# Block-sparse attention and a ResMLP in one kernel: pair 5's q and k transposed by DMA, the opening and the weave's lists placed anew

## The chip, the cores and the metric

The kernel runs on one core of a Trainium2 chip. The metric is the device time of one execution in microseconds. A core has five engines with instruction queues of their own: TensorE (PE; its weight loads are shown as PEld), VectorE (DVE), ScalarE (ACT), GpSimd (POOL) and SyncE (SP, which only issues DMAs here). POOL and SP issue nearly all DMAs; each executes its queue strictly in the order written.

## The reference

```python
def _attn_ref(q, k, v, sampled_blocks):          # q, k, v: 4 x 8 x 768 x 64
    scores = (1 / sqrt(D)) * q @ k.transpose
    mask = |block_i - block_j| <= 1 or first/last block row or column
           or one of 3 sampled blocks per row of blocks (blocks of 32)
    attn = softmax(where(mask, scores, -1e9))
    return attn @ v

def _moe_ref(x, ...):                            # x: 4 x 768 x 512, heads side by side
    a1 = alpha1 * x + beta1
    tok = einsum('ts,bsd->btd', w_tok, a1)
    u = x + lam * tok
    a2 = alpha2 * u + beta2
    ch = relu(a2 @ w_ch1) @ w_ch2                # 512 -> 2048 -> 512
    return u + lam * ch
```

## The kernel before

**Tiling.** The eight heads of each of the four batches are taken two by two: 16 *pairs* (`NP` = 4 to a batch). The scores of a pair are computed key by key in nine *units* (`WIDE`, `HALF`): a unit is 128 x 1024 scores in PSUM, two or four matmuls (`emit_qk`, L569), then one Exp of 1024 or two of 512 columns on ACT into a tile `eT` (`emit_exp`, L587; six such tiles). `emit_pv` (L616) and `emit_pv_keys` (L639) multiply the result with v (matmuls of 65 columns), `emit_finish` (L656, L657) divides, on VectorE, into `x_sb`, and `emit_a1pp` (L673, L674) makes `a1`, mostly on POOL.

**Two kinds of pairs.** Pairs 0 to 4 (`MP` = 5) carry the mask inside the matmul, with 24 more rows. Pairs 5 to 15 keep q and k of both heads on 64 rows each (`qhTs`, `khTs`), two matmuls run side by side, and the mask is a multiply on VectorE after the Exp (`emit_keep`, L604), for which POOL first spreads the mask out (`emit_mask01`, L505).

**Transposes.** q and k must stand with the head dimension on the partitions. Pair 0 goes through `emit_tps0` (L467), pairs 1 to 4 through `emit_tps` (L479, L485): six TensorE transposes into PSUM, then VectorE copies. Pairs 6 to 15 go through `emit_tdma` (L530 for k, L535 and L538 for q): DMA transposes on SP's queue. Pair 5 goes through `emit_tph` (L519; copies L521 and L524 to L526) or `emit_tdma`, as `TDM[1]` says (`TDM[0]` is read by nothing).

**The MLP.** `job_tok` and `job_tok2` multiply with the transposed `w_tok` (`emit_wtok_t`, L761) and add to `x_sb`; `emit_cast` makes bf16 copies; these are transposed by TensorE (`job_ut`, L829, L830) or by DMA (`emit_udma` L844, `emit_uscale` L853). `job_f1` (L867, four matmuls of 384 columns, then Relu on ACT, L874) and `job_f2` (L886, four matmuls of 512 columns; after four such jobs the add L895 and the store) are the channel MLP; 128 f1 jobs and 92 f2 jobs, and the last tile in two parts (L906). `w2b` is scaled by `lam` in 16 VectorE multiplies (`lam0` to `lam15`, L748).

**What sets the order.** `tc.manual_schedule()`: each engine executes in the order in which the code emits.

- *The opening*: 45 units, one after the other (pairs 0 to 4). In unit `s` the code emits the scores, the Exp, the jobs of `PLAN` whose number is `s` to `s`.49, from unit 42 on `POUR[s - 42]` f1 jobs, then the PV pieces of unit `s - 2`, then the jobs of `PLAN` from `s`.5. A number is a place in the order, no time.
- *The weave*: a list of strings for each third of a pair (`W1` for pairs 5 to 7, `W2` for four pairs and run twice, `W3` the tail). `q` emits three units' scores and the first Exp, `x` another Exp, `k` a mask multiply, `p` a PV piece, `f` and `g` an f1 and f2 job, `T` a `job_tok2`, `s` starts the MLP work of a finished couple of pairs, `d` and `v` are `emit_udma` and `emit_uscale`, `L` loads q, k and v of a later pair (POOL, L304), `Q` and `K` are the DMA transposes of the next pair, `Y` copies v (L315), `0`, `1`, `2` emit what `PLAN` holds for that place.
- `A1V` says for pairs 0 to 3 which `emit_a1pp` go to VectorE instead of POOL.
- `emit_warm` (L449) issues matmuls of 512 columns on a tile of zeros: eight ahead of everything, two more ahead of unit 0, and the jobs `warm0`, `warm1`, `warm2` (one, two and one).

PSUM has two tiles `sp` for scores, three `mm` for nearly everything else and one `op` for PV results and warm matmuls. The constants of each vector (`parts`, POOL, L696 to L700) are spread over the partitions by `emit_bcast` (L705, L714, L716).

```python
    for s in range(N1):
        emit_qk(s)
        emit_exp(s)
...
        fns(s, False)
        if s >= OPEN:
            for _ in range(POUR[s - OPEN]):
                todo["f"].pop(0)()
        if s >= LAG:
            emit_pvs(s - LAG)
        fns(s, True)
```

Of the kernel before, what the change touches and what calls it, by code (L numbers as in the profile page):

```python
# [71 lines left out]
]  # L72
WEAVE = W1 + W2 * (B - 2) + W3
ENG = {
# [19 lines left out]
    "layv00": 0.29,
    "wtkl": 0.42,
    "warm1": 0.49,
    "loadv2": 0.58,
    "layk01": 1.22,
    "layq01": 1.25,
    "mask_cols": 1.5,  # L100
    "rows1": 2.08,
    "tps0": 2.52,
    "parts": 2.83,
    "mask1": 2.94,
    "w1_0": 2.96,
    "warm2": 3.04,
    "warm0": 3.31,
    "tq1": 3.8,
# [1 line left out]
    "rows2": 4.5,  # L110
    "tk1": 4.82,
    "lv1": 5.01,
    "bcast0": 5.1,
    "rows3": 5.84,
    "loadk3": 6.08,
    "bcast2": 6.12,
    "loadv3": 7.02,
    "mask3": 7.41,
# [2 lines left out]
    "bcast1": 8.8,
    "loadq3": 9.23,
    "a1pp0": 9.37,
    "w1_2": 9.64,
    "w1_1": 10.3,
    "columns": 11.32,
    "wt2": 11.35,
    "wt1": 11.76,
    "wt5": 12.19,
    "lv2": 12.84,  # L130
    "wt4": 13.01,
    "wt0": 13.43,
    "loadv4": 13.94,
    "w1_3": 14.3,
    "tq2": 14.44,
    "loadq4": 14.54,
    "wt3": 15.31,
    "columns_use": 16.32,
    "tk2": 16.6,
    "tok0_0": 17.05,  # L140
    "tok0_1": 17.4,
    "tk3": 18.13,
    "loadk4": 18.23,
    "tok0_2": 20.0,
    "tq3": 20.4,
    "mask8": 20.72,
    "loadk5": 20.73,
    "mask2": 20.89,
    "tok0_3": 21.32,
    "tok0_4": 22.02,  # L150
    "lv3": 22.91,
    "mask6": 22.94,
    "mask0": 23.62,
    "tok0_5": 23.87,
    "loadq5": 24.3,
    "tok1_0": 24.53,
    "mask4": 24.64,
    "w2_0": 24.82,
    "mask7": 25.08,
    "lv4": 25.4,  # L160
    "tok1_1": 25.6,
    "tok1_2": 27.2,
    "loadv5": 27.53,
    "tok1_3": 27.74,
    "tok1_4": 28.91,
    "tok1_5": 29.7,
    "w2_2": 29.98,
    "mask5": 30.09,
    "tq4": 30.41,
    "mask15": 30.72,  # L170
    "udma0": 30.82,
    "tk4": 31.72,
    "udma1": 31.9,
    "w2_1": 32.02,
    "tq5": 32.51,
    "mask9": 32.65,
    "tok2_0": 33.91,
    "tk5": 34.64,
    "usc0": 34.69,
    "tok2_1": 34.88,  # L180
    "mask14": 34.9,
    "mask13": 35.48,
    "tok2_2": 35.71,
    "mask11": 35.79,
    "tok2_3": 36.37,
    "lam16": 37.24,
    "mask17": 37.68,
    "w2_3": 37.7,
    "mask16": 37.75,
    "tok2_4": 37.77,  # L190
    "mask10": 37.9,
    "tok3a_0": 38.34,
    "tok3a_1": 38.43,
    "tok2_5": 38.51,
    "tok3a_2": 38.52,
    "tok3a_3": 38.85,
    "tok3a_4": 39.48,
    "tok3b_0": 39.51,
    "tok3b_1": 39.52,
    "tok3b_2": 39.53,  # L200
    "tok3b_3": 39.54,
    "ut2": 39.85,
    "tok3a_5": 40.02,
    "mask12": 40.23,
    "tok3b_4": 40.23,
    "usc1": 40.28,
    "lv5": 40.42,
    "ut3_0": 40.8,
    "tok3b_5": 41.21,
    "cast3": 42.22,  # L210
    "lam2": 42.25,
    "lam3": 43.09,
    "ut3_1": 43.63,
    "lam1": 44.85,
    "lam10": 44.92,
    "lam9": 45.25,
    "lam7": 45.27,
    "lam0": 45.32,
    "lam11": 45.58,
    "lam6": 45.9,  # L220
    "lam13": 46.09,
    "lam5": 47.61,
    "lam14": 47.82,
    "lam4": 47.9,
    "lam8": 49.72,
# [6 lines left out]
def kernel(  # L232
# [416 lines left out]
    def emit_finish(i, w):  # L649
        b, hp = i // NP, i % NP  # L650
        if (hp, w) == (0, 0):
            x_sbs[b] = ap_.tile([P, NT, DM], FP, name="x_sb", tag="x_sb", bufs=3)
# [4 lines left out]
        nc.vector.tensor_tensor(  # L657
            out=x_sbs[b][:, :, ts(2 * hp + w, D)],
            in0=op[:, :, 0:D],
            in1=rcp[:].unsqueeze(2).broadcast_to([P, NT, D]),  # L660
            op=ALU.mult,
        )
# [520 lines left out]
```

## Time and profile before

| what | value |
|---|---|
| median of 3 runs | 303.80 us (303.79 to 303.88) |
| the profiled execution | 304.01 us |
| its span, first to last instruction | 302.2 us |
| busy in the span: TensorE, ACT, VectorE, POOL | 296.6, 214.5, 191.6, 111.6 us |
| granted TensorE clock | 1.00 |
| DMA moved | 31.37 MB, 104 GB/s mean |

The page gives busy times, the chain of work that ended last (followed back from the last instruction to what released each) and groups of instructions by line. Rows of the views name the line, the engine, the operation, the tile written and the tiles read, the count, and in brackets what ended an idle stretch of the engine. The end of a matmul is modelled, so TensorE counts as busy in short waits too; where its pieces in the chain are longer than their kind usually is, it waited. One execution was profiled; it lay 0.2 us over the median.

### The profile page before, as it was taken

The page shows a single profiled execution, that of the slowest core. Times are in us where ns is not written, and L with a number is a line of the kernel's source. Part 1 is how long each engine was busy: PE and PEld are TensorE (multiplying, and loading weights), DVE is VectorE, ACT ScalarE, POOL GpSimd, SP SyncE. Part 2 cuts the span into 40 slices and gives each one's busy share as a digit, 9 for nine tenths or more (in the row PEclk, how much of TensorE's full clock was granted, in tenths as well). Part 3 has the DMA queues.
Part 4 walks back from the last instruction along what each step waited for, and adds up shares of the span by engine and source line. Part 5 has one row for each costly group of instructions (what it writes and reads, how often), then busy time and mean ns, then how long its engine had stood idle before and what let it go on. Part 6 is the DMA issues. An engine that isn't in the chain of part 4 may idle for free.

```text
span 302.2 us, 7215 instructions
## 1 busy us (share of the span) xinstructions
PE 296.6 (98%) x2997; PEld 184.5 (61%) x2997; DVE 191.6 (63%) x373; ACT 214.5 (71%) x314; POOL 111.6 (37%) x147
## 2 busy tenths in 40 slices
PE   8999999999999999999999999999999999999995
PEld 3677888655567656565665556565675664555543
DVE  4887789887658899845477779854476872000012
ACT  4899997999879775889778774889868600663310
POOL 5989589344338432613407501603105300000000
PEclk9999999999999999999999999999999999999999
DMA  7999999827296797960746793880510004100011
GB/s 200 214 194 205 196 155 168 134 55 125 72 130 114 113 138 121 128 160 2 119 74 110 117 169 87 125 168 0 63 38 16 37 35 121 37 0 35 37 69 69
DMA packets 57891, 31.37 MB, mean 104 GB/s; under 512 B 37952, under 2 KB 54740, under 8 KB 57732
## 3 DMA queue, kind: packets, MB, share of 16 engines
q0 software_dynamic: 16608, 14.22, 32.1%
q1 hardware_dynamic: 40784, 16.15, 25.3%
q10 hardware_dynamic: 468, 0.55, 0.5%
q8 instruction: 23, 0.38, 0.5%
q14 instruction: 8, 0.07, 0.1%
HBM read 29.86 MB, written 6.29 MB: 120 GB/s over the span
## 4 chain that ended last, share of the span: by engine, by line
PE 96%; ACT 3%; issue 0%; DVE 0%
PE mm L867 28%; PE mm L886 27%; PE sp L569 10%; PE op L639 8%; PE mm L802 8%; PE mm L569 4%; PE mm L778 3%; ACT eT L587 3%; PE op L616 2%; PE op L449 2%; PE mm L906 1%; PE mm L616 1%; PE mm L479 1%; PE mm L761 1%; PE mm L829 0%
## 5 line engine op out<-in xcount | busy, mean ns | idle before, releaser
L587 ACT ACTIVATE eT<-sp,expb 128x1024 f16<-128x1024 f32 x111 | 118.3, 1117 | 4.4 <-PE sp L569 3.9
L874 ACT ACTIVATE hts<-mm 128x384 bf16<-128x384 f32 x128 | 62.0, 495 | 48.0 <-PE mm L867 47.2
L867 PE MATMUL mm<-uT,w1b 128*128 128x384 bf16 x512 | 92.6, 326 | 0.0
L604 DVE TENSOR_TENSOR eT<-eT,mask 128x1024 f16<-128x1024 f16 x99 | 74.1, 771 | 26.9 <-ACT eT L587 26.6
L886 PE MATMUL mm<-w2b,hts 128*128 128x512 bf16 x368 | 87.7, 379 | 0.0
L673 POOL TENSOR_TENSOR a1pp<-x_sb,vbc 128x384 bf16<-128x384 f32 x27 | 32.7, 1210 | 123.0 <-DVE x_sb L657 121.8
L867 PEld LDWEIGHTS <-w1b 128*128 128x128 bf16 x512 | 48.1, 98 | 35.0 <-issue 3.4
L886 PEld LDWEIGHTS <-hts 128*128 128x128 bf16 x368 | 34.1, 98 | 38.6 <-issue 4.0
L587 ACT ACTIVATE eT<-mm,expb 128x512 f16<-128x512 f32 x66 | 41.7, 685 | 18.6 <-PE mm L569 18.3
L895 DVE TENSOR_TENSOR ot<-x_sb,mm 128x512 f32<-128x512 f32 x23 | 15.7, 684 | 45.4 <-PE mm L886 45.4
L639 PEld LDWEIGHTS <-eT 128*128 128x128 f16 x792 | 29.6, 98 | 8.7 <-issue 1.5
L639 PE MATMUL op<-vext,eT 128*128 128x65 f16 x792 | 31.7, 194 | 0.0
L674 POOL TENSOR_TENSOR a1pp<-a1pp,vbc 128x384 bf16<-128x384 bf16 x27 | 27.8, 1029 | 2.1
L569 PE MATMUL sp<-qTs,kTs 88*128 88x512 bf16 (+1 forms) x120 | 27.1, 327 | 0.9 <-ACT eT L587 0.7
L802 PE MATMUL mm<-a1pp,wtokT 128*128 128x256 bf16 x216 | 25.6, 273 | 0.0
L802 PEld LDWEIGHTS <-wtokT 128*128 128x128 bf16 x216 | 20.7, 98 | 4.2 <-ACT hts L874 0.8
L569 PE MATMUL sp<-qhT,khT 64*128 64x256 bf16 (+1 forms) x176 | 19.7, 322 | 0.0
L616 PEld LDWEIGHTS <-eT 128*128 128x128 f16 x360 | 14.9, 97 | 4.2 <-PE op L449 0.8
L569 PEld LDWEIGHTS <-khT 64*128 64x128 bf16 x264 | 10.5, 94 | 10.8 <-issue 6.8
L814 DVE TENSOR_TENSOR x_sb<-x_sb,mm 128x512 f32<-128x512 f32 x18 | 12.3, 686 | 7.1 <-PE mm L802 6.8
L657 DVE TENSOR_TENSOR x_sb<-op,rcp 128x384 f32<-128x384 f32 x28 | 15.6, 557 | 1.0
L820 DVE CAST ubf<-x_sb 128x256 bf16<-128x256 f32 (+1 forms) x44 | 13.7, 347 | 0.9
(92 smaller groups left out, 222.8 us busy)
## 6 DMA issues: line engine op xcount, KB each, us to landing
out_dram<-ot SPq DMA_DIRECT2D x23, 256.0 KB, 2.0
qpad<-in_q_dram POOLq DMA_DIRECT2D x15, 192.0 KB, 4.0
kr<-in_k_dram POOLq DMA_DIRECT2D x15, 192.0 KB, 5.7
vr<-in_v_dram POOLq DMA_DIRECT2D x15, 192.0 KB, 6.0
w1b<-in_moe_w_ch_dram POOLq DMA_DIRECT2D x4, 512.0 KB, 10.3
w2b<-in_moe_w_ch_dram POOLq DMA_DIRECT2D x4, 512.0 KB, 7.4
hts<-in_moe_w_tok_dram POOLq DMA_DIRECT2D x1, 1152.0 KB, 10.4
x_sb<-in_k_dram ACTq DMA_DIRECT2D x2, 192.0 KB, 3.2
```

The costliest lines, as they stand in the source:

```text
L569: nc.tensor.matmul(sp[jj][:, dst], lhsT, rhs, start=True, stop=True, skip_group_check=True,)
L587: nc.scalar.activation(dst, at, AF.Exp, bias=expb[:], scale=SCALE)
L604: nc.vector.tensor_mul(out=e, in0=e, in1=keep)
L616: nc.tensor.matmul(op[0][:, o, :], ets[u][:, jj, h * QB + n * P : h * QB + n * P + P], vexts[i % NVB][:, w, 2 * jp + jj, :], start=op[1] == 0,
L639: nc.tensor.matmul(op[0][:, o, :], ets[u][:, jj, h * QB + n * P : h * QB + n * P + P], vexts[i % NVB][:, w, 2 * jp + jj, :], start=op[1] == 0,
L673: eng.tensor_tensor(out=dst, in0=x_sbs[b][:, :, cols], in1=bc[0], op=ALU.mult)
L674: eng.tensor_tensor(out=dst, in0=dst, in1=bc[1], op=ALU.add)
L802: nc.tensor.matmul(ps[:, o], wtokT[:, os_, ts(2 * n + o, P)], a1pps[i][:, os_, :], start=(os_ == 0 and o == 0), stop=(os_ == NT - 1 and o ...
L867: nc.tensor.matmul(ps[:, 0:QC], w1b[:, dk, ts(n, P)], uTs[b][:, dk, ts(c, QC)], start=(dk == 0), stop=(dk == 3),)
L874: nc.scalar.activation(hts[(b, c)][:, n, :], ps[:, 0:QC], AF.Relu)
L886: nc.tensor.matmul(ps[:], ht[:, nk, ts(o % 3, P)], w2b[:, nk, :], start=(nk == 0), stop=(nk == NH - 1),)
L895: nc.vector.tensor_tensor(out=ot[:], in0=x_sbs[b][:, o, :], in1=ps[:], op=ALU.add)
```

## The change

Pair 5's `tk5` and `tq5` call `emit_tdma`: three DMA transposes on SP's queue instead of twelve transposes on TensorE and four copies on VectorE. All else is a new order of the same instructions: `A1V` moves one `emit_a1pp` of pair 1 from POOL to VectorE or back (entry 0 is read by nothing; entries 2 and 3 change places), `POUR` emits no, nine and no f1 jobs in units 42 to 44 (a negative count is an empty range), the lists of the weave are written anew, and 131 of the 134 numbers of `PLAN` change.

```diff
-TDM = [1, 0]
-A1V = [1, 0, 0, 1, 0, 0, 0, 1]
-POUR = [3, 1, 1]
+TDM = [1, 1]
+A1V = [0, 0, 1, 0, 0, 0, 0, 1]
+POUR = [-21, 9, -78]
 W1 = [
-    "q f Y x f 0 f p k 1 f k f p x 2 f f k f f",
-    "q L f x Q f f f k p x f p 0 k 1 p k 2",
-    "q x g x f k k f 0 g 1 g k 2 K",
-    "q Y Q k p K g p x x 0 f 1 s k 2 p k L f",
-    "q 0 f x x g 1 g g k p k k 2",
-    "q k s g p f x 0 f k 1 T x f p 2 k",
-    "q 0 1 f p x k 2 p K T x L k p k",
-    "q f x f 0 x T 1 p 2 Y k p k k Q",
-    "q x f 0 k k g p x 1 s 2 g k d g",
+    "q Q f x 0 f f p f f 1 k f x f 2 f k p g k",
+    "q k 0 Y g g p p x 1 x K k 2 k",
+    "q g L 0 1 k x f f x p 2 s f f f k k p",
+    "q x k 0 p Y p K g x k g k L 1 2",
+    "q p g 0 s f p 1 x k x Q 2 g k k f T",
+    "q x p k T k x 0 1 f p 2 k f",
+    "q K T Q p d p s k L 0 1 2 x x k k f f",
+    "q f x f f k k g p p 0 x 1 f k Y g f p d g f 2",
+    "q 0 k g g x 1 x g f k 2 k",
 ]
 W2 = [
-    "q 0 p p p f d L x K f k v g 1 Q v g k x g g k 2",
-    "q x 0 k f x g s 1 k 2 T T p p k T",
-    "q d Y k p x g 0 1 2 g d g k x v p k",
-    "q k L g x k 0 p g g 1 x p k 2 Q v",
-    "q g x p g 0 x f f f Y k 1 f k 2 k f",
-    "q 0 f k p x k f p f f f x 1 p p K f k f 2",
-    "q f f x f f k 0 1 Q Y x p k g g 2 k s",
-    "q 0 g g s k x f f 1 f 2 x k L f k p p",
-    "q T f T T k 0 1 x x k K f f 2 f k p f f",
-    "q p p p d s k x L d 0 x K k g k Y 1 f f 2 g",
-    "q 0 x k Q g x 1 g p k 2 k p",
-    "q k x v 0 1 p g k x k f g f g 2",
+    "q 0 Q K v p p v x p x 1 g g k f k f k 2 Y f L s",
+    "q 0 x T T 1 k T g x p g 2 k k",
+    "q p 0 d 1 g k p g x k 2 x g d k",
+    "q k p p g K x g x v k k L p 0 v 1 2",
+    "q g k x 0 1 Y 2 k f f f f p p x f f k",
+    "q f 0 f k s x f p 1 f k f 2 x Q f f p f k f",
+    "q k Q 0 x k 1 p f Y g g L x 2 p k",
+    "q g x g f s 0 k 1 f k 2 x T K p p p k",
+    "q f x f 0 1 x f k T k k f p 2",
+    "q k T 0 p Q x k p L x 1 k s 2 f Y",
+    "q f K f k x g p 0 d g 1 g d x v k f k 2 g",
+    "q k v p p 0 1 x f f x 2 f g k g k",
 ]
 W3 = [
-    "p p p f g v f s g T T T g g d g g g g d g g v g v g g f f f f f f",
-    "f f f f f f f f f f f f g f f g f g f g f f g g f g f f g f f g g g f g",
-    "f f g g g g g g g g g g g g",
+    "p p p",
+    "f g s g T T T f d g v g g f d",
+    "g g g v g g g g g g f f f f f f f f g g f f g g f f f f f f f f g f f g f g g f f g f g g g f f f f f g g g f g f f g g g g g g g g",
 ]
```

Of `PLAN`, the entries that the prediction speaks of (before and after):

```diff
-    "warm1": 0.49,    "warm2": 3.04,    "warm0": 3.31,
+    "warm1": 27.17,   "warm0": 28.18,   "warm2": 44.07,
-    "bcast0": 5.1,    "rows1": 2.08,    "tps0": 2.52,    "parts": 2.83,
+    "bcast0": 4.68,   "rows1": 1.14,    "tps0": 2.99,    "parts": 2.39,
-    "loadk3": 6.08,   "loadv3": 7.02,   "loadq3": 9.23,  "a1pp0": 9.37,
+    "a1pp0": 9.68,    "loadq3": 9.8,    "loadv3": 9.93,  "loadk3": 10.27,
-    "w1_0": 2.96,     "w1_2": 9.64,     "w1_1": 10.3,    "w1_3": 14.3,
+    "w1_0": 15.3,     "w1_1": 29.93,    "w1_2": 34.16,   "w1_3": 37.56,
-    "tk3": 18.13,     "columns_use": 16.32,
+    "tk3": 21.97,     "columns_use": 28.85,
-    "udma0": 30.82,   "udma1": 31.9,    "tq5": 32.51,    "tk5": 34.64,
+    "udma0": 34.49,   "udma1": 35.98,   "tq5": 41.91,    "tk5": 41.99,
-    "usc0": 34.69,    "usc1": 40.28,    "ut2": 39.85,    "ut3_0": 40.8,   "ut3_1": 43.63,
+    "usc0": 38.06,    "usc1": 38.4,     "ut2": 41.67,    "ut3_0": 42.26,  "ut3_1": 44.2,
```

More of the change, by code (lines that the diff above doesn't have):

```diff
@@ L93 @@
 PLAN = {
[L94 to L108, printed above, removed]
-    "layv01": 4.3,
[L110 to L118, printed above, removed]
+    "wtkl": 0,
@@ L119 @@
+    "layk01": 0.2,
+    "layq01": 0.5,
+    "layv00": 0.6,
+    "loadv2": 0.95,
+    "rows1": 1.14,
+    "parts": 2.39,
+    "tps0": 2.99,
+    "mask_cols": 3.13,
+    "tq1": 3.23,
+    "layv01": 4.3,
+    "bcast0": 4.68,
+    "mask1": 4.85,
+    "rows2": 5.44,
+    "tk1": 6.79,
+    "bcast1": 7,
+    "mask14": 7.61,
     "loadk2": 8.21,
     "loadq2": 8.52,
[L121 to L225, printed above, removed]
@@ L226 @@
-    "lam12": 49.8,
-    "lam15": 50.13,
+    "mask12": 8.56,
+    "w2_0": 8.93,
+    "bcast2": 9.06,
+    "a1pp0": 9.68,
+    "loadq3": 9.8,
+    "mask16": 9.82,
+    "lv1": 9.89,
+    "loadv3": 9.93,
+    "loadk3": 10.27,
+    "mask2": 10.88,
+    "rows3": 10.97,
+    "wt2": 11.16,
+    "wt4": 11.97,
+    "lv2": 11.98,
+    "wt1": 12.42,
+    "wt0": 12.44,
+    "wt5": 12.97,
+    "tq2": 13.36,
+    "mask6": 14.26,
+    "wt3": 14.29,
+    "columns": 15.02,
+    "tk2": 15.18,
+    "w1_0": 15.3,
@@ new lines @@
+    "tok0_0": 16.7,
+    "tok0_1": 16.83,
+    "lv3": 17.04,
+    "loadv5": 17.17,
+    "loadq4": 17.24,
+    "mask11": 17.72,
+    "tok0_3": 18.08,
+    "w2_3": 18.19,
+    "loadv4": 18.38,
+    "mask0": 18.61,
+    "loadk4": 19,
+    "tok0_2": 19.49,
+    "tok0_4": 20.72,
+    "tok0_5": 20.74,
+    "tk3": 21.97,
+    "tq3": 22.12,
+    "loadq5": 22.27,
+    "w2_2": 22.78,
+    "w2_1": 23.21,
+    "tok1_0": 23.59,
+    "tok1_1": 24.32,
+    "loadk5": 24.33,
+    "tok1_3": 25.42,
+    "mask17": 25.92,
@@ new lines @@
+    "tok1_2": 25.97,
+    "warm1": 27.17,
+    "lam16": 27.45,
+    "lam13": 27.59,
+    "warm0": 28.18,
+    "columns_use": 28.85,
+    "lam15": 28.97,
+    "tok1_4": 29.02,
+    "mask15": 29.17,
+    "tok1_5": 29.17,
+    "mask10": 29.72,
+    "mask5": 29.8,
+    "w1_1": 29.93,
+    "lv5": 30.29,
+    "tk4": 31.06,
+    "mask8": 32.14,
+    "tok2_3": 32.57,
+    "lv4": 33.56,
+    "tok2_4": 33.78,
+    "tq4": 33.83,
+    "tok2_0": 33.99,
+    "w1_2": 34.16,
+    "tok2_1": 34.25,
+    "udma0": 34.49,
@@ new lines @@
+    "mask3": 34.73,
+    "tok2_2": 35.11,
+    "lam8": 35.56,
+    "udma1": 35.98,
+    "lam5": 37.36,
+    "mask9": 37.4,
+    "w1_3": 37.56,
+    "tok2_5": 37.65,
+    "tok3a_0": 37.97,
+    "usc0": 38.06,
+    "tok3a_1": 38.31,
+    "tok3a_3": 38.39,
+    "usc1": 38.4,
+    "tok3a_2": 38.69,
+    "tok3a_4": 38.91,
+    "tok3b_0": 40.29,
+    "tok3b_3": 40.34,
+    "tok3b_1": 40.5,
+    "tok3a_5": 40.62,
+    "tok3b_2": 40.75,
+    "mask4": 40.82,
+    "tok3b_4": 41.53,
+    "ut2": 41.67,
+    "tq5": 41.91,
@@ L228 @@
+    "tk5": 41.99,
+    "tok3b_5": 42.09,
+    "ut3_0": 42.26,
+    "lam10": 42.94,
+    "lam4": 43.19,
+    "lam9": 43.48,
+    "lam2": 43.54,
+    "cast3": 43.87,
+    "lam7": 43.91,
+    "warm2": 44.07,
+    "lam12": 44.09,
+    "ut3_1": 44.2,
+    "mask7": 44.23,
+    "mask13": 44.96,
+    "lam0": 45.45,
+    "lam3": 45.58,
+    "lam11": 46.99,
+    "lam1": 47.55,
+    "lam6": 47.81,
+    "lam14": 48.35,
 }
```

## The prediction

> **What bounds the kernel now.** I read three views: busy shares and the chain of work that ended last on the page, busy time by stretch, and the pieces of that chain in order of time.
>
> ```profile
> PE 296.6 (98%) x2997; PEld 184.5 (61%) x2997; DVE 191.6 (63%) x373; ACT 214.5 (71%) x314; POOL 111.6 (37%) x147
> ...
> PE 96%; ACT 3%; issue 0%; DVE 0%
> ```
>
> TensorE is busy 98% of the span and 96% of the chain is TensorE's. Busy is modelled there, so the stretches say more:
>
> ```profile
> 6.50:19.30 12.80, 11.82 (x156) 8.34 (x155) 10.62 (x28) 11.53 (x12) 11.01 (x21) 1.00 1.15 200
> 19.30:59.00 39.70, 39.67 (x651) 32.05 (x649) 34.14 (x71) 36.70 (x38) 30.98 (x45) 1.00 1.14 175
> 59.00:240.00 181.00, 181.00 (x1827) 109.34 (x1826) 130.62 (x238) 146.64 (x223) 65.54 (x68) 1.00 0.57 96
> ```
>
> The columns after the stretch are the busy times of PE, weight load, DVE, ACT and POOL. From 59 to 240 us (the weave) TensorE is busy 181.0 of 181.0, from 19.3 to 59 (the rest of the opening) 39.67 of 39.7. Before that it is not. The chain shows what bounds there:
>
> ```profile
> 6.93 2.13 ACT eT L587 x2
> ...
> 9.97 0.39 PE op L449
> ...
> 11.88 1.94 ACT eT L587 x2
> ...
> 13.92 0.80 ACT eT L587
> ...
> 15.91 2.25 ACT eT L587 x2
> ...
> 18.20 0.60 PE sp L569 x4
> 18.80 0.67 PE mm L761 x12
> 19.47 0.43 PE sp L569 x2
> ```
>
> Up to 18.2 us the chain runs over the Exp of L587, unit after unit; from 18.2 on it never leaves TensorE. So the rule for this change: up to 18 us what counts is when Exps can start; from there on, each TensorE instruction removed is time won, each one added is time lost, a reordering wins only where TensorE waits now, and it loses wherever a new wait appears.
>
> **The change part by part.**
>
> *Removed: 12 transposes of pair 5 (L519), with four VectorE copies.*
>
> ```profile
> 24.44 0.15 PE mm L729
> 24.60 0.44 PE mm L479 x6
> ...
> 28.46 0.59 PE sp L569 x4
> ...
> 34.72 0.59 PE sp L569 x2
> ...
> 39.07 0.50 PE sp L569 x2
> ...
> 42.10 0.34 PE mm L519 x6
> ...
> 43.77 0.34 PE mm L519 x6
> ...
> 54.02 1.95 PE mm L867 x12
> ```
>
> Both sixes stand in the chain with 0.34 us: **-0.68 us**. The copies are off the chain and count for nothing by themselves; VectorE was 34.14 of 39.7 busy there.
>
> *Added: three DMA transposes on SP's queue.* They stand behind the two of `udma0` and `udma1` and ahead of pair 6's.
>
> ```profile
> 34.31 7.18 SPq L844 DMA_TRANSPOSE uraw<-ubf  x2
> 57.73 1.21 SPq L535 DMA_TRANSPOSE qhT<-qpad  x1
> ...
> 30.99 0.72 POOL L304 DMA_DIRECT2D qpad<-in_q_dram  x1
> ...
> DMA to landing us min/median/max: 3.0/4.3/5.6
> ```
>
> SP runs ahead of TensorE: it is free from 41.5 to 57.7 us. Pair 5's q is fetched at 31 us (last row but one). So the three transposes go out from about 42 us, 1.2 us each, and with 5.6 us at most to land they are there by 52; the first matmul that needs them comes after 59. Nothing waits: 0. If that cover were gone (SP held up), each us beyond 59 would be a us of time.
>
> *Moved: four warm matmuls* (`warm0` to `warm2`, L449). Before, two stand behind unit 0's scores and two behind unit 3's, while TensorE waits anyway; now they stand in units 27, 28 and 44, inside the TensorE-bound stretch. A 512-column matmul there takes a quarter of the four in the next row's pace, 1.73 / 8 = 0.216 us:
>
> ```profile
> 74.50 1.73 PE mm L886 x8
> ```
>
> 4 x 0.216 = **+0.86 us**. What their leaving wins at the start is bounded by:
>
> ```profile
> 9.53 0.81 PE L449 MATMUL op<-warm 128*128 128x512 bf16 x2
> ...
> 11.60 0.42 POOL L700 TENSOR_TENSOR parts<-rest,part 12x128 bf16<-12x128 f32 x1
> ...
> 11.88 10.50 ACT L587 ACTIVATE eT<-sp,expb 128x1024 f16<-128x1024 f32 x10 [0.82 <-PE sp L569]
> ...
> 12.27 0.60 PE L569 MATMUL sp<-qTs,kTs 88*128 88x512 bf16 x2
> ```
>
> ACT idles 0.82 us ahead of unit 4's Exp because the second pair of warm matmuls and q's transposes hold that unit's scores back. Without them unit 4 can come some 0.6 us earlier. But now `bcast0` (four matmuls, L705) stands ahead of unit 5's scores, and it reads `parts`, which POOL finishes at 12.02 (11.60 + 0.42). So unit 5's scores start at about 12.3, where they start now (12.27), and from there Exps follow each other at 1.0 us (10.50 us for ten) to unit 11 at 18.2. I take 0; the ends are -0.8 (the whole idle time won) and +0.1.
>
> [...]
>
> ```profile
> 1.19 3.59 PE L449 MATMUL op<-warm 128*128 128x512 bf16 x8 [1.19 <-DVE expb L377]
> ```
>
> The first eight run at half the later pace, and the pace stays up once it is there; a fall back is priced as rival C.
>
> *Moved: f1 jobs.* `POUR` gave 3 + 1 + 1 jobs to the opening, now 0 + 9 + 0 (a negative count pours none). Four more, 4 x 0.65 = 2.6 us (12 matmuls in 1.95, four to a job), lengthen the opening and shorten the weave by the same: 0.
>
> *Waits that may close.* In the chain above, pieces exceed their usual size: 0.15 + 0.10 around L729, 0.15 at 28.46 (0.59 where four take 0.44), 0.16 at 34.72 and 0.07 at 39.07 (0.43 is usual): 0.63 us. L729 is issued again in unit 28 and should keep its 0.2. The others came where a unit had too little TensorE work to cover an Exp; with two warm matmuls and the `tok` jobs laid anew the units of that stretch now hold 0.9 to 1.3 us each. **-0.4 us**, between -0.6 and 0.
>
> *Waits that may open.* I add the known durations along the new order.
>
> ```profile
> L830 DVE TENSOR_SCALAR uT<-mm,ab2T 128x384 bf16<-128x384 bf16 (+1 forms) x3 | 1.6, 536 | 0.1
> ...
> L793 DVE TENSOR_TENSOR x_sb<-x_sb,mm 128x384 f32<-128x384 f32 x8 | 4.4, 548 | 1.9 <-PE mm L778 1.9
> ```
>
> First f1 job, unit 43: its fourth matmul reads `uT` of pair 3. Between `ut2` and this job TensorE has two score units, 0.43 each, two half jobs of 0.17 and a PV piece of 0.12, 1.3 us, plus 0.48 for the job's first three matmuls; VectorE has two L830 and one L793, 1.6 us, and 0.2 us of latency at each end: a wait of about 0.2.
>
> ```profile
> 59.47 1.26 ACT L587 ACTIVATE eT<-mm,expb 128x512 f16<-128x512 f32 x2
> ...
> L604 DVE TENSOR_TENSOR eT<-eT,mask 128x1024 f16<-128x1024 f16 x99 | 74.1, 771 | 26.9 <-ACT eT L587 26.6
> ...
> L657 DVE TENSOR_TENSOR x_sb<-op,rcp 128x384 f32<-128x384 f32 x28 | 15.6, 557 | 1.0
> ...
> PEld L639 <- DVE eT L604: 0.8, 3, 0.3
> ```
>
> Weave, first three pairs: the lists place PV pieces earlier. The first PV piece of pair 6 stands now at the head of the fifth list (`q p g ...`), before in the middle of it. Behind its scores TensorE has q 0.86, two PV pieces 0.74, two f2 jobs 1.73 and the next q 0.86: 4.2 us. What it needs: 0.4 to the Exp, 1.15 for the two halves, 1.1 for unit 55's Exp (2.65 so far), while VectorE does mask, `lay` and finish; then that unit's mask multiply, 0.77, behind the finish (0.56 + 0.19): 4.2 to 4.5. So 0 to 0.3 us is missing. In the kernel before, the last row says, TensorE's weight loads waited three times for a mask multiply, 0.8 us together, so such edges exist there too, and cost nothing visible. I find one more place as tight in the sixth list, and the second and fourth are short (3.3 us of TensorE for 3.15 of Exp). Since such edges cost nothing visible before, I take 0.2 for all, the end near 0; with the first f1 job **+0.4 us** in total, bounds 0 and 2.0.
>
> *Covered moves.* POOL: `a1pp0` now stands ahead of pair 3's loads and waits for `vbc`:
>
> ```profile
> 17.78 0.99 POOL L673 TENSOR_TENSOR a1pp<-x_sb,vbc 128x384 bf16<-128x384 f32 x1 [1.18 <-DVE vbc L716]
> ...
> DMA to landing us min/median/max: 3.3/5.3/10.9
> ...
> w1b<-in_moe_w_ch_dram POOLq DMA_DIRECT2D x4, 512.0 KB, 10.3
> ```
>
> So these loads go out at 20 to 22.5 us, not at 14 to 16, land by 28 at the median, and `tk3` needs k at about 30.7: hidden, 2.7 us lost at the slowest landing. The last piece of `w1b` goes out at about 49 us, lands at 60, and job 12 of f1 comes at about 64. The `lam` multiplies, masks and `lay` jobs stay on VectorE and POOL, neither of them the bound. Tail: the same instructions end it; the list puts six f2 jobs between `usc` of pair 15 and the first f1 job that reads it: 0.
>
> **Sum**, against the profiled execution's 304.01 us (span 302.2, 1.8 around it): -0.68 + 0.86 + 0 - 0.4 + 0.4 = +0.2, so 304.2; the profiled execution lies 0.2 above the median of the runs shown, 303.80, so the median comes to **304.0 us**. What the transposes give, the warm matmuls take.
>
> **The rivals.**
> *A, the start is won:* if unit 5 isn't held by `parts` (other ops of POOL end earlier) or TensorE takes it in its stride, the 0.8 us of idle ACT goes: 304.0 - 0.8 = 303.2, down to 302.8 with no new wait. For: the idle time is in the chain. Against: 12.02.
> *B, slower, the PV pieces pulled forward become TensorE's bound in the weave:* place, the heads of the lists; price, up to 0.3 us at two places of the first nine lists and as much at two places of the twelve lists that run twice, 6 x 0.3 = 1.8 us, in place of the 0.2: 304.0 - 0.2 + 1.8 = 305.6. It makes the kernel slower by over 0.2% from 0.4 us of waits above what I took (304.0 + 0.4 against 303.8 + 0.6). For: 4.2 us offered against 4.2 to 4.5 needed. Against: the kernel before has such edges and no visible wait.
> *C, the clock falls back at the start* (with the warm matmuls gone TensorE has work for some two thirds of the time there): at half speed 2.4 us of work in a stretch as long as the eight warm matmuls, 3.59 us, take 4.8, about 1.2 more: 305.2. [...]
> *D, pair 5's transposes come late:* held until 57.7, where pair 6's go out now, they would land at about 65, and pair 5's scores are wanted at 59.0 + 2.6 = 61.6: +3.5, 307.5. Against: SP's idle 16 us.
>
> **How the numbers follow.** Forecast, within 0.2% (0.6 us, about what a measurement of this kernel can tell from no change): 0.53. A 0.13, B 0.28, C 0.03, D 0.03. So faster 0.13, same 0.53, slower 0.34. The range reaches from A's 303.1 to 305.4, where B's six waits stand near their full price; what lies outside (A with no new wait, B beyond six waits, D) I put at 0.2.
>
> **What would show it.** L519 gone, khT and qhT landing by 52 us; `op<-warm` in the chain near 38 us; unit 5's Exp within 0.2 us of 12.9 and unit 12's scores at 19.3 (A is wrong then); the first scores of pair 5 at 59.0 + 2.6, within 0.4; in the stretch up to 240 us pieces of L639 or L569 above their 0.37 to 0.43 would be B's. A first f1 job that waits over 0.5 us, or VectorE waiting for a landing, would make me wrong.

## The result, and where the time went

The kernel after takes 311.38 us (median of 6 runs, 308.85 to 313.39) against 303.80 us (303.57 to 304.62): a ratio of 1.0244, 95% interval 1.0215 to 1.0273. It is 7.6 us slower, and its runs spread over 4.5 us where those of before spread over 1.0. My 304.0 was wrong, and so was the range. The experiments below are told by the median and the ends of all their runs: the comparison of ratios leaves out runs over 1.5% above the fastest of a kernel, and here that spread is the effect.

The profiled execution took 313.39 us, span 311.5. The page's chain of the kernel after, by engine:

```profile
PE 296.3 (95%) x2958; PEld 183.9 (59%) x2985; DVE 191.5 (61%) x369; ACT 215.2 (69%) x314; POOL 112.6 (36%) x147
...
PE 82%; DMA 8%; POOL 4%; DVE 3%; issue 1%; ACT 1%; SPq 0%; POOLq 0%
```

TensorE is busy for as long as before, but the chain, 96% TensorE's then, now has 8% of DMA. By stretch, with the columns of before's rows (the last three are the granted clock, the DMA engines' busy share, where more than 1 means that transfers lie over one another, and GB/s):

```profile
6.50:19.30 12.80, 11.18 (x154) 8.14 (x152) 10.55 (x27) 11.92 (x12) 10.51 (x21) 1.00 1.13 198
19.30:59.00 39.70, 38.48 (x613) 30.76 (x613) 34.23 (x71) 35.94 (x38) 31.52 (x45) 1.00 1.34 162
59.00:240.00 181.00, 173.87 (x1753) 104.95 (x1771) 126.55 (x229) 143.35 (x216) 64.49 (x66) 0.98 0.59 101
```

TensorE is idle for 1.2 us from 19 to 59 us and for 7.1 behind it, and for the first time the clock isn't 1.00. The share of the DMA engines ahead of 59 us rose from 1.14 to 1.34, while what they move fell from 175 to 162 GB/s. TensorE's part of the timeline shows the stops (in brackets the idle time and what ended it):

```profile
57.85 2.77 PE L867 MATMUL mm<-uT,w1b 128*128 128x384 bf16 x16 [0.58 <-ACT hts L874]
61.67 0.82 PE L867 MATMUL mm<-uT,w1b 128*128 128x384 bf16 x4 [1.05 <-DMA w1b<-in_moe_w_ch_dram]
...
67.94 0.61 PE L569 MATMUL mm<-qhT,khT 64*128 64x512 bf16 x2 [3.96 <-DMA khT<-kr]
```

The longest is the first matmul of pair 5: it waits 4 us for the k that DMA transposes. SP's queue shows when those transposes went out:

```profile
31.20 10.49 SPq L844 DMA_TRANSPOSE uraw<-ubf  x2
41.79 2.61 SPq L535 DMA_TRANSPOSE qhT<-qpad  x1
44.49 7.04 SPq L538 DMA_TRANSPOSE qhT<-qpad  x1
51.63 5.72 SPq L530 DMA_TRANSPOSE khT<-kr  x1
66.36 1.21 SPq L535 DMA_TRANSPOSE qhT<-qpad  x1
```

They left SP from 41.8 us as predicted, but took 15.4 us to be issued instead of 3.6, and the chain has khT landing 16.3 us after its start. Behind the wait, the chain's pieces run slow:

```profile
51.63 16.26 DMA khT<-kr
67.89 0.05 issue
67.94 0.61 PE mm L569 x2
68.54 0.85 PE sp L569 x6
69.40 3.83 PE mm L867 x12
...
77.84 0.32 PE mm L569 x2
78.16 0.43 PE sp L569 x6
...
84.56 1.95 PE mm L867 x12
```

The same three pieces take 2.70 us once the pace is back; here they took 5.29. The granted clock says why:

```profile
64.00:68.00 4.00, 0.07 (x2) 0.07 (x4) 0.83 (x3) 0.14 (x1) 0.00 (x0) 0.77 0.73 114
68.00:70.00 2.00, 2.00 (x11) 0.71 (x12) 0.06 (x1) 1.27 (x2) 0.00 (x0) 0.50 1.12 166
70.00:74.00 4.00, 4.00 (x24) 2.14 (x23) 2.00 (x4) 2.37 (x4) 0.00 (x0) 0.63 0.24 55
74.00:78.00 4.00, 3.95 (x31) 2.19 (x31) 0.95 (x3) 3.24 (x6) 0.11 (x1) 1.00 0.00 0
```

While TensorE idled, the clock fell to 0.50 and stayed there until 73 us. So this execution's loss adds up: 4.0 (khT) + 2.6 (half clock) + 1.05 (w1b) + 0.6 (f1 behind ACT) come to 8.2 of the 9.3 us between the spans. Two smaller waits make most of the rest, each on one row of the table of waits: L778 for `x_sb` (0.5), and at 201 us an f1 job for `uT` of L853 (0.5).

### The profile page after: what moved, and what is told of

The parts are those of the page before. It is cut to its first block, busy times and chain, and to the rows that moved or that the text cites. A ratio compares the mean times of both kernels' runs of the same rounds, so it can differ in the third digit from the quotient of the medians.

```text
span 311.5 us, 7156 instructions
## 1 busy us (share of the span) xinstructions
PE 296.3 (95%) x2958; PEld 183.9 (59%) x2985; DVE 191.5 (61%) x369; ACT 215.2 (69%) x314; POOL 112.6 (36%) x147
## 4 chain that ended last, share of the span: by engine, by line
PE 82%; DMA 8%; POOL 4%; DVE 3%; issue 1%; ACT 1%; SPq 0%; POOLq 0%
PE mm L867 26%; PE mm L886 23%; PE op L639 8%; PE mm L802 8%; PE sp L569 8%; DMA khT<-kr 5%; PE mm L569 3%; DMA uraw<-ubf 2%; PE mm L778 1%; PE op L616 1%; PE mm L906 1%; PE mm L616 1%; DMA x_sb<-in_q_dram 1%; POOL kr L304 1%; POOL qpad L304 1%
## 5 line engine op out<-in xcount | busy, mean ns | idle before, releaser
L867 PE MATMUL mm<-uT,w1b 128*128 128x384 bf16 x512 | 94.1, 331 | 2.2 <-DMA w1b<-in_moe_w_ch_dram 1.1
L604 DVE TENSOR_TENSOR eT<-eT,mask 128x1024 f16<-128x1024 f16 x99 | 77.0, 802 | 29.2 <-ACT eT L587 27.8
L886 PE MATMUL mm<-w2b,hts 128*128 128x512 bf16 x342 | 84.6, 379 | 1.6 <-issue 0.5
L639 PEld LDWEIGHTS <-eT 128*128 128x128 f16 x792 | 29.1, 98 | 9.5 <-issue 4.0
L639 PE MATMUL op<-vext,eT 128*128 128x65 f16 x792 | 31.6, 194 | 0.0
L674 POOL TENSOR_TENSOR a1pp<-a1pp,vbc 128x384 bf16<-128x384 bf16 x27 | 28.7, 1061 | 2.5 <-DVE vbc L716 0.5
L569 PE MATMUL mm<-qhT,khT 64*128 64x512 bf16 (+1 forms) x88 | 13.1, 335 | 4.1 <-DMA khT<-kr 4.0
## 6 DMA issues: line engine op xcount, KB each, us to landing
w1b<-in_moe_w_ch_dram POOLq DMA_DIRECT2D x4, 512.0 KB, 15.7
```

Of the source, the lines that this page charges most:

```text
L569: nc.tensor.matmul(sp[jj][:, dst], lhsT, rhs, start=True, stop=True, skip_group_check=True,)
L604: nc.vector.tensor_mul(out=e, in0=e, in1=keep)
L639: nc.tensor.matmul(op[0][:, o, :], ets[u][:, jj, h * QB + n * P : h * QB + n * P + P], vexts[i % NVB][:, w, 2 * jp + jj, :], start=op[1] == 0,
L674: eng.tensor_tensor(out=dst, in0=dst, in1=bc[1], op=ALU.add)
L867: nc.tensor.matmul(ps[:, 0:QC], w1b[:, dk, ts(n, P)], uTs[b][:, dk, ts(c, QC)], start=(dk == 0), stop=(dk == 3),)
L886: nc.tensor.matmul(ps[:], ht[:, nk, ts(o % 3, P)], w2b[:, nk, :], start=(nk == 0), stop=(nk == NH - 1),)
```

## The theories

*Theory 1*: the loads of w1b, moved from 12 to 24 us to as late as 47.5 us, crowd the DMA engines just when pair 5's transposes go out. *Theory 2*: pair 5's DMA transposes come late by themselves. After the first runs I gave up both for *theory 3*: ahead of some 57 us the DMA engines (busy share 1.14 from 19 to 59 us in the kernel before) are as much a bound as TensorE, so any traffic that is added makes whatever lands last late, and a wait taken away at one place comes back at another.

## Experiments: which part of the change costs the time

**The transposes alone, in the kernel before.**

```diff
-TDM = [1, 0]
+TDM = [1, 1]
```

> The kernel before, with one edit: pair 5's q and k by DMA (three DMA transposes) instead of twelve TensorE transposes; all places unchanged. Theory 1 (the weights of f1, w1b, loaded late, crowd the DMA engines just when pair 5's transposes go out): with w1b early as here the transposes land before 59 us, the time is 303.1 (-0.68 for the transposes) to 303.8. Theory 2 (DMA transposes of pair 5 are late in any case, since the engines are full from 36 to 57 us in the kernel before too): the first scores of pair 5 wait 2 to 4 us, with 2.7 us more at half clock if the wait is over 3.5 us: 306 to 310.

Measured: 308.73 us (305.13 to 310.95). Nothing else is changed, and most of the loss is there: theory 2's number, not theory 1's. The waits of this kernel:

```profile
PEld L569 <- DMA khT<-kr: 3.2, 1, 3.2
PE mm L569 <- DMA khT<-kr: 3.0, 1, 3.0
...
DVE vext L315 <- DMA vr<-in_v_dram: 2.4, 1, 2.4
```

**The same, with the weights' loads of the kernel after** (`w1_0` to `w1_3` and `w2_0` to `w2_3` take their numbers from the kernel after).

```diff
-TDM = [1, 0]
+TDM = [1, 1]
-    "w1_0": 2.96,  "w1_1": 10.3,  "w1_2": 9.64,  "w1_3": 14.3,
+    "w1_0": 15.3,  "w1_1": 29.93, "w1_2": 34.16, "w1_3": 37.56,
-    "w2_0": 24.82, "w2_1": 32.02, "w2_2": 29.98, "w2_3": 37.7,
+    "w2_0": 8.93,  "w2_1": 23.21, "w2_2": 22.78, "w2_3": 18.19,
```

> The kernel before, with pair 5 by DMA and, besides, the loads of w1b and w2b at the places that they have in the kernel after (w1b last). Theory 1: the transposes land after 64 us, TensorE waits 3 to 5 us and then runs at half clock: 309 to 312, and f1 jobs wait for w1b. Theory 2 (the place of the weights doesn't matter): the same as with the transposes alone, within 1 us.

Measured: 314.69 us (312.38 to 316.42), with 6.3 us of waiting for khT. The place of the weights adds 6 us, so theory 2 isn't enough either.

**The weights' loads of the kernel after alone**, pair 5 by TensorE.

> The kernel before, pair 5 by TensorE as there, with only the loads of w1b and w2b at the places of the kernel after (w1b last). Theory 1 (the late weights matter through the DMA transposes of pair 5, that they crowd): 303.8 to 305, what is lost is a wait for w1b or for pair 5's k. Rival (the late weights cost by themselves): 307 to 309, since the transposes alone made 308.7 and both together 314.7.

Measured: 309.26 us (308.86 to 312.77). That is the rival's number, and a miss for theory 1: pair 5 has no DMA transposes to be crowded, and still 5 us are lost. What is late now is another transfer, pair 5's q from memory; behind the wait the clock is at 0.50 for 3.4 us:

```profile
PEld L519 <- DMA qpad<-in_q_dram: 3.2, 1, 3.2
PE mm L519 <- DMA qpad<-in_q_dram: 3.1, 1, 3.1
```

**The kernel after with the weights back** (`w1`, `w2` and `lam0` to `lam15` with their numbers of before; one of the sixteen multiplies, `lam8`, then comes after the first f2 job that reads its rows).

```diff
-    "w1_0": 15.3,  "w1_1": 29.93, "w1_2": 34.16, "w1_3": 37.56,
+    "w1_0": 2.96,  "w1_1": 10.3,  "w1_2": 9.64,  "w1_3": 14.3,
-    "w2_0": 8.93,  "w2_1": 23.21, "w2_2": 22.78, "w2_3": 18.19,
+    "w2_0": 24.82, "w2_1": 32.02, "w2_2": 29.98, "w2_3": 37.7,
```

> The kernel after, with the loads of w1b and w2b and the multiplies of w2b by lam back at their places of the kernel before. Theory 1: the waits for w1b (1.9 us), for khT (4.0) and the half clock behind it (2.7) go: 303 to 305. Theory 2: khT is still late, 4.0 and 2.7 us stay: 309 to 311.

Measured: 304.71 us (304.34 to 308.03): the wait for khT, the wait for w1b and the half clock are gone, though pair 5 is still transposed by DMA. The nine f1 jobs of unit 43 find their w1b and keep TensorE at work, so that no matmul waits for khT.

**The kernel after with pair 5 by TensorE**, ahead of the nine f1 jobs.

```diff
-TDM = [1, 1]
+TDM = [1, 0]
-    "tq5": 41.91, "tk5": 41.99,
+    "tq5": 43.4,  "tk5": 43.45,
```

> The kernel after, with pair 5's q and k by TensorE again (ahead of the nine f1 jobs of unit 43, when q and k have landed). Both theories: the wait for khT and the half clock go (-6.7), 0.7 us of transposes come: 305.4 from 311.4; the wait for w1b (1.2 us at 60 us) stays, or shrinks if the DMA transposes are what slowed w1b. If it stays near 311, the wait for khT only hid another one (w1b's last pieces, pair 6's loads).

Measured: 307.91 us (306.41 to 309.69), 2.5 above what both theories gave. The wait for khT and the half clock are gone; new ones are my own doing: at this place the transposes hold two of the three `mm` tiles until VectorE's copies, and two f1 jobs wait 0.6 us each. That is half of the 2.5; the rest is open.

## Experiments: is it the traffic?

**The kernel before with pair 5 by DMA and w2b early**, so that all weights are under way ahead of 35 us.

```diff
-TDM = [1, 0]
+TDM = [1, 1]
-    "w2_0": 24.82, "w2_1": 32.02, "w2_2": 29.98, "w2_3": 37.7,
+    "w2_0": 8.93,  "w2_1": 23.21, "w2_2": 22.78, "w2_3": 18.19,
```

> The kernel before, with pair 5 by DMA and the loads of w2b at their early places of the kernel after, so that all weights are fetched by some 40 us. If the full DMA engines (w2b and pair 6's loads at 37 to 57 us) are what makes the three transposes late: they land before 59 us, 303.1 to 304. If the transposes are late for another reason (they wait for one another, or for q and k): 307 to 309 as with the transposes alone (308.7).

Measured: 307.64 us (306.99 to 307.84). A miss for the first case, and a telling one: khT now costs 0.3 us, and in its place pair 4's k, whose load had to stand behind w2b, is late:

```profile
PEld L479 <- DMA kr<-in_k_dram: 3.4, 1, 3.4
PE mm L479 <- DMA kr<-in_k_dram: 3.3, 1, 3.3
...
PEld L569 <- DMA khT<-kr: 0.4, 1, 0.4
```

**The kernel after with w1b early as well.**

```diff
-    "w1_0": 15.3,  "w1_1": 29.93, "w1_2": 34.16, "w1_3": 37.56,
+    "w1_0": 2.96,  "w1_1": 10.3,  "w1_2": 9.64,  "w1_3": 14.3,
```

> The kernel after, with the loads of w1b at their early places of the kernel before and w2b as in the kernel after (early). Full engines as the cause: no wait for khT, none for w1b, clock 1.00: 303.5 to 304.9 (304.7 with w1b early and w2b late). If it is the number of bytes before 60 us that counts, not their place: 307 or more.

Measured: 308.35 us (308.06 to 310.43): the second case's number. TensorE waits for neither khT nor w1b; the k of pairs 3 and 4 comes late (2.2 us at L479), and with the stops around it the clock falls here too, to 0.50 from 46.2 to 49.6 us. But the bytes alone don't explain it: up to 60 us this kernel moved 197 GB/s, 11.8 MB, and the kernel with the weights back, which took 304.71, moved 189 GB/s, 11.3 MB. What differs is the order, with w2b ahead of those loads of k, and the places of `lam0` to `lam15`. The same holds for the weights' loads alone, where no byte is added to the kernel before.

**More traffic that nobody reads.** The kernel before, pair 5 by TensorE, and beside it the same three DMA transposes into the other buffer:

```diff
+        if i == MP:
+            jobs_of[f"tk{i}"] = lambda i=i: (emit_tph(i, "k"), emit_traffic(i, "k"))
+            jobs_of[f"tq{i}"] = lambda i=i: (emit_tph(i, "q"), emit_traffic(i, "q"))
```

> The kernel before, pair 5 by TensorE as there, with three more DMA transposes of pair 5's q and k at the same two places, written to the other buffer where nothing reads them before pair 6's own transposes overwrite them: pure traffic. Theory 3 (from 19 to 57 us the DMA engines are the bound, so 0.6 MB more of slow traffic delays whatever lands last, also PE's own instructions): 305.5 to 309, though nobody waits for these transposes. Rival (the loss is only the first scores' wait for khT): 303.8 to 304.2.

Measured: 308.39 us (303.30 to 311.15, 12 runs, two of them at 303.3 and 303.4, ten from 307.2 up). Theory 3's case: the traffic alone costs 4.6 us at the median, though nobody waits for these transposes, but in two of the twelve runs it costs nothing. The profiled run (308.77) shows by what: TensorE stops for 1.0 us within a group of the `job_tok` matmuls that are L778 in the kernel before (of which more below), and pair 6's v lands 14.6 us after its issue, so VectorE waits 6.3 us ahead of its copy, and the mask multiplies that stand behind the copy in the code run from 68.7 us on. In this kernel's lines and its chain:

```profile
52.04 14.60 DMA vr<-in_v_dram
66.63 0.02 issue
66.66 0.04 DVE vext L315
...
73.45 1.81 DVE eT L616 x3
75.27 0.05 issue
75.32 0.62 PE op L651 x8
```

**Other transposes taken from the DMA engines.** The kernel before with pair 5 by DMA, and a2 of pairs 0 and 1 by TensorE.

```diff
-UTD = [1, 1]
-TDM = [1, 0]
+UTD = [0, 0]
+TDM = [1, 1]
```

> The kernel before, pair 5 by DMA (three transposes, some 0.6 MB), but the a2 of pairs 0 and 1 transposed by TensorE (two DMA transposes, 0.4 MB, fewer; twelve TensorE transposes, 0.68 us, more). Theory 3 (the sum of the traffic counts): most of the traffic is given back, the transposes of pair 5 start 7 us earlier on SP's queue: 303.6 to 304.6. Rival (the transposes of pair 5 are slow in themselves, whatever else is under way): 307 to 309.

Measured: 304.64 us (nine runs from 304.13 to 305.41, two at 310.9). Where the traffic is given back, so is most of the time. TensorE has twelve transposes more for a2 and twelve fewer for pair 5, so the 0.8 us that are left over 303.8 are not explained by their number and stay open. The profiled run is one of the two outliers, and it has a stop of its own (below); the other wasn't profiled.

**The place in SP's queue.** The kernel before with pair 5 by DMA, its transposes between `udma0` and `udma1`.

```diff
-TDM = [1, 0]
+TDM = [1, 1]
-    "tq5": 32.51, "tk5": 34.64, "loadq5": 24.3,
+    "tq5": 31.86, "tk5": 31.87, "loadq5": 23.9,
```

> The kernel before, pair 5 by DMA, its transposes put on SP's queue between the two transposes of a2 (udma0 and udma1) instead of behind them, and the load of pair 5's q a little earlier. If only their place in the queue makes khT late: 303.1 to 304. Theory 3 (the sum of the traffic counts, so something else is late instead: the second a2, or PE's instructions): 305 to 309.

Measured: 314.96 us (312.94 to 318.13). khT is in time, and worse is late: the second a2 transpose, on which VectorE's next cast into `ubf` waits.

```profile
DVE ubf L820 <- DMA uraw<-ubf: 9.6, 1, 9.6
POOL kr L304 <- DMA khT<-kr: 6.4, 1, 6.4
```

**The traffic taken away.** Three of the four pieces of w2b are set to a constant on POOL instead of being loaded (3 MB less to read; the channel MLP is computed with that), first with pair 5 by TensorE, then by DMA:

```diff
     def emit_w2_load(g):
+        if g:
+            nc.gpsimd.memset(w2b[:, ts(g, 4), :], 0.01)
+            return
         nc.gpsimd.dma_start(
```

> The kernel before with three of the four pieces of w2b not loaded but set to a constant on POOL (the channel MLP is computed with that; it leaves 3 MB of reading out), pair 5 by TensorE. It is the yardstick for the next run. Both theories: 303.5 to 303.9, as the kernel before.

> The same (three pieces of w2b set to a constant on POOL), with pair 5 by DMA. Theory 3 (the full DMA engines make the transposes and PE's instructions late): with the engines freed nothing waits, the time is the yardstick's less the 0.68 us of transposes, 303.0 to 303.3, and the spread of several us goes. Rival (the transposes are late or costly whatever else is under way): 306 to 309.

Measured: 304.05 us (303.83 to 304.58) and 303.75 us (303.48 to 304.32). With the engines freed the transposes by DMA win 0.3 us, less than the 0.68 expected, no run strays, and behind the first 15 us TensorE waits for no landing. From the two kernels' DMA views of the same stretch, 41.4 to 48.5 us, comes how long the packets of the three transposes take; first the second kernel, with them:

```profile
q1 hardware_dynamic: 3096, 0.77, 82.8%
q0 software_dynamic: 480, 0.39, 37.9%
```

and the first, without:

```profile
q0 software_dynamic: 454, 0.37, 35.8%
q1 hardware_dynamic: 800, 0.20, 21.9%
```

Packets, MB, and share of the 16 engines over 7.1 us: (82.8 - 21.9)% x 7.1 = **4.3 us of all sixteen engines' packet time** for 0.57 MB. That is the load that my sum had at 0. It is an upper estimate of what the engines do for them, since packets lie over one another here too (the shares with them add up to more than 1), and the runs don't tell whether the engines themselves or the memories behind them are what is full.

**The kernel after without w1b's traffic** (three of four pieces of w1b set to a constant, f1 computed with that).

```diff
     def emit_w1_load(g):
+        if g:
+            nc.gpsimd.memset(w1b[:, :, ts(g, DM)], 0.01)
+            return
         nc.gpsimd.dma_start(
```

> The kernel after with three of the four pieces of w1b not loaded but set to a constant on POOL (f1 is computed with that). Theory 3: the waits for khT, for w1b and the half clock go, and what is left is the prediction's own sum: 303.6 to 304.8, with a small spread. Rival (the new lists and the other moves cost several us by themselves): 306 or more.

Measured: 304.19 us (303.78 to 305.53). Everything else of the change is in it, the lists, the opening, the DMA transposes, and it is 0.3 us over the kernel before. The prediction's own sum comes out once the DMA engines have room, though in part by luck, since two of its terms were measured at other sizes (below) and the two of 0.4 us for waits that close and open were priced by no run.

## Experiments: TensorE's stop, the clock, and the terms of the sum

**Keeping TensorE at work in the wait** (eight matmuls on zeros ahead of pair 5's first scores).

```diff
+    wps = mm_tile()
+    for _ in range(8):
+        nc.tensor.matmul(wps[:], warm[:, 0:P], warm[:], start=True, stop=True)
     for p, text in enumerate(WEAVE):
```

> The kernel after, with eight matmuls of 512 columns on zeros put ahead of pair 5's first scores, where TensorE waits some 4 us for khT in the kernel after. Theory A (the half clock behind that wait is caused by TensorE's idling): the idle stretch is cut to some 2.4 us, the clock stays 1.00 and 2 to 2.7 us go: 308.9 to 309.5 from 311.4, and the spread of the runs is smaller. Theory B (the half clock has another cause, or the wait alone makes the whole loss): 311.4, or up to 1.7 us more.

Measured: 311.14 us (310.09 to 313.23), no gain that can be told from 311.38. In the profiled run the wait for khT is only 0.4 us, but TensorE had stopped elsewhere, within a group of six matmuls of L778 and with no releaser that the profile shows, and the clock fell there:

```profile
56.65 0.23 PE L778 MATMUL mm<-a1pp,wtokT 128*128 128x64 bf16 x2 [3.56 <-issue]
```

```profile
56.00:58.00 2.00, 1.35 (x18) 1.09 (x19) 0.68 (x1) 0.18 (x1) 0.00 (x0) 0.86 1.42 103
58.00:60.00 2.00, 2.00 (x15) 1.39 (x13) 1.89 (x6) 1.40 (x2) 0.20 (x1) 0.50 1.22 195
60.00:62.00 2.00, 2.00 (x12) 1.03 (x11) 2.00 (x3) 1.59 (x3) 1.92 (x3) 0.78 1.26 194
```

So the experiment doesn't isolate the clock's share: a new stop took the place of the old one, and at 200 us an f1 job waits 1.5 us for `uT` of L853.

**More f1 jobs ahead of pair 5** (the kernel before with pair 5 by DMA).

```diff
-TDM = [1, 0]
+TDM = [1, 1]
-POUR = [3, 1, 1]
+POUR = [3, 1, 6]
```

> The kernel before, pair 5 by DMA, and five more f1 jobs (3.2 us of TensorE) in unit 44, ahead of pair 5's first scores, w1b early as there. Theory 3: TensorE has work while the DMA engines catch up, the wait for khT (3.2 us) is filled: 303.3 to 305. Rival (what is late are the instructions, the loads of pair 6, or whatever follows): 307 to 309.

Measured: 307.03 us (306.09 to 307.84). Half a miss: the wait for khT is gone from the profiled run (span 304.3), as theory 3 has it, but VectorE waits 5.5 us for pair 6's v, and in the weave, where the f1 jobs are now missing, TensorE's PV matmuls (L639) wait for VectorE, for 0.4, 0.3, 0.5 and 0.3 us at 94 to 104 us.

**The warm matmuls.** The kernel after with the weights and the `lam` multiplies back, the four at their places of before:

```diff
-    "warm1": 27.17, "warm0": 28.18, "warm2": 44.07, "lam8": 49.72,
+    "warm1": 0.49,  "warm0": 3.31,  "warm2": 3.04,  "lam8": 47.95,
```

> The kernel after with the weights and the lam multiplies back (304.7 in an earlier run), one lam multiply (lam8) a unit earlier so that all of w2b is scaled in time, and the four warm matmuls back at their places of the kernel before. By the prediction's step, 0.86 us of TensorE time leave the stretch that TensorE bounds: 303.8 to 304.0. Rival (the warm matmuls stood in time that TensorE lost anyway to waits for the DMAs, or the start gets slower by what they bring): 304.5 to 305.

Measured: 305.38 us (303.75 to 308.06, 12 runs), against 304.71: inconclusive, the spread is larger than the term. Then without the crowd, the kernel before without w2b's traffic, the four at their places of the kernel after:

```diff
-    "warm1": 0.49,  "warm0": 3.31,  "warm2": 3.04,
+    "warm1": 27.17, "warm0": 28.18, "warm2": 44.07,
```

> The kernel before with three of the four pieces of w2b set to a constant on POOL (304.05 in an earlier run; the channel MLP is computed with that), and the four warm matmuls at their places of the kernel after, in units 27, 28 and 44. The prediction's step: four times 0.216 us in a stretch that TensorE bounds, nothing won at the start: 304.9. Rival (the units there wait for an Exp anyway, or the start is won): 303.3 to 304.3.

Measured: 304.64 us (304.28 to 305.17) against 304.05: +0.6. In the traces the Exps run 0.4 us earlier up to 36 us and 0.5 us later from 60 us on: something is won at the start, and about 0.9 is lost behind it.

**The lists.** The kernel after without w1b's traffic, with the weave's lists and `POUR` of before.

```diff
-POUR = [-21, 9, -78]
+POUR = [3, 1, 1]
...
-    "q Q f x 0 f f p f f 1 k f x f 2 f k p g k",
+    "q f Y x f 0 f p k 1 f k f p x 2 f f k f f",
...
```

> The kernel after with three of the four pieces of w1b set to a constant on POOL (304.19 in an earlier run; f1 is computed with that), and the weave's lists and the f1 jobs poured into units 42 to 44 as in the kernel before. If the new lists cost what their trace shows (waits of 0.3, 0.45 and 0.68 us at 102, 111 and 192 us): 302.8 to 303.3. If the lists are neutral, as the prediction has it within 0.2: 303.9 to 304.4.

Measured: 308.48 us (307.10 to 309.89), far from both. With three f1 jobs in unit 42 instead of nine in unit 43, TensorE comes to the transposes of `ut3_1` while VectorE is still at four multiplies of w2b ahead of their cast:

```profile
57.09 3.23 DVE L751 TENSOR_TENSOR w2b<-w2b,lam_bcb 128x512 bf16<-128x512 bf16 x4
60.24 0.54 DVE L823 CAST ubf<-x_sb 128x384 bf16<-128x384 f32 x1
```

It waits 2.8 us, and the clock falls to 0.50 until 66.7 us. The run doesn't price the lists; it shows that this opening and the old lists with their `POUR` don't fit each other.

## Why the prediction was wrong, step by step

- **The step that failed**: "the three transposes go out from about 42 us, 1.2 us each, and with 5.6 us at most to land they are there by 52 ... Nothing waits: 0." Both figures are of DMA transposes, but of a calm stretch: the rows of `qhT` begin at 57.7 us. I looked at whose queue was free (SP's) and not at what executes it: the share of the DMA engines, 1.14 in the very rows that I quoted from 19 to 59 us, was in front of me. Adding transposes with 4.3 us of all sixteen engines' packet time to that stretch, and nothing else, cost 4.9 us at the median; in the kernel after they took 15.4 us to issue and khT landed at 67.9, and TensorE waited 4.0 us. With the weights back the nine f1 jobs covered the wait, and the whole change cost 0.8 (304.71 against 303.93).
- **Covered moves** failed for the same reason: "lands at 60, and job 12 of f1 comes at about 64". The median landing of w1b went from 10.3 to 15.7 us, and I missed that the ninth job of unit 43 already reads the third piece, which went out at 45.7 us. The price: 1.05 us, and the traffic at 42 to 60 us. The median in the kernel after:

```profile
w1b<-in_moe_w_ch_dram POOLq DMA_DIRECT2D x4, 512.0 KB, 15.7
```

- **Rival D** named the wait (khT, +3.5) with the wrong condition, SP held up, and 0.03. **Rival C**'s clock does fall, which costs 2.6 us, not at the thinner start (1.00 from 6.5 to 59 us) but at the wait that D makes. I had them as cases that exclude each other; in the kernel after the fall begins within the wait.
- **-0.68 for the transposes**: 0.3 measured (304.05 to 303.75; between 0.1 and 0.6 by the spread of the two sets of eleven runs). The timelines of the two kernels without w2b's traffic, first by TensorE, then by DMA, reach the unit behind the second six at nearly the same time; the matmuls ahead of it wait 0.17, 0.13 and 0.24 us where the transposes had filled the time, so most of them hid in it. I had taken a place in the chain for a price.

```profile
43.99 0.60 PE L569 MATMUL sp<-qTs,kTs 88*128 88x512 bf16 x2
```

```profile
43.93 0.59 PE L569 MATMUL sp<-qTs,kTs 88*128 88x512 bf16 x2
```

- **+0.86 for the warm matmuls**: 0.6 measured (between 0.3 and 0.8 by the spread); about 0.86 less the 0.4 of a start that in that kernel isn't held by `bcast0`.
- **The start, 0**: right within 0.3 us, and for the reason given. In the kernel after `parts` ends at 11.73 us, `bcast0` follows, unit 5's Exp starts at 12.63 against 12.90, and the 0.7 us that unit 4 won are mostly gone again:

```profile
11.30 0.43 POOL parts L700
11.73 0.04 issue
11.77 0.38 PE mm L705 x4
12.15 0.45 PE sp L569 x2
```

- **Sum without the DMA engines**: +0.2 predicted, +0.3 with w1b's traffic gone (304.19 against 303.88). Rival B's waits at the PV pieces don't show as stops of TensorE in the kernel after. What the new lists do bring is another one: an f1 job that waits 0.5 us for `uT` of L853, at 201 us in the kernel after and at 193 without w1b's traffic.

## What to carry to other kernels

Before a transfer is counted as hidden, add up the DMA engines' busy share over the stretch in which it runs. Here it was 1.14 from 19 to 59 us, and transfers with 4.3 us of packet time cost 4.6 and 4.9 us, paid by what landed last (pair 6's v, khT). With w2b's traffic gone (share 0.92 from 36 to 48 us and 0.02 from 48 to 54, against 1.15 and 1.02 in the kernel before), the same transposes cost nothing: 303.75 against 304.05. Most of it wasn't paid where TensorE had other work, as the run with the weights back shows (0.8 us), and with w2b early the wait went from khT to pair 4's k (3.3 us). SP's queue stood idle where the transposes were added, which said nothing on that, and the 5.6 us of a calm stretch were no bound: khT took 16.3. If undoing each part moves the wait to another tile instead of removing it, look for the shared resource, and take traffic away (or add some that nobody reads) to see it.
